# Output projection in eight pairs by seven products, and the down weight's sums made by accumulating transfers in DRAM

## The chip, the core and the metric

The kernel runs on one core of a Trainium2 chip. The metric is the device time of one execution in microseconds (us). Before the change three timed runs took 740.05, 740.07 and 741.11 us, median 740.07.

The engines are named as the profile names them: PE multiplies matrices (PEld loads its weights), DVE is the vector engine, ACT the activation engine, POOL the general engine, and SP issues most of the transfers. Each engine works through its own list of instructions in the order of the program, and waits where an operand is not ready. What stands behind a waiting instruction on the same engine waits with it.

## The reference, cut to what matters

The input `x` has 2048 rows of 640. After a layer norm it goes through two branches:

```
xn  = layernorm(x)
qkv = xn @ wqkv                  # 32 heads of 20, window of 8 positions, dilation 2
o   = windowed attention(qkv)    # 2048 x 640
s   = o @ wo                     # the output projection
h   = (xn @ w_gate) * (xn @ w_up)   # 2048 x 1536
g   = silu(h @ w_down)           # the down projection
out = x + s * g
```

All is float32. For PE each operand is cut into a high and a low part, and a product is the sum of three (high by high, high by low, low by high).

## The kernel before, in words

The rows are cut into sixteen tiles of 128 (NT = 16). The work goes through PE in this order: the query/key/value products beside the first gate and up products (to about 272 us), the gate and up products in groups (to about 520 us), the output projection (520 to 586 us), and the down projection (586 us to the end). Attention itself runs on DVE and POOL beside the products of the first two parts, and its results `o` go to DRAM, as do `h` and later `s`.

**Seven products instead of eight.** Where two tiles are taken together as a pair, rows and the inner dimension are halved into blocks A11, A12, A21, A22, the weight into B11 to B22, and a scheme of seven block products with sums S1 to S4 of the A blocks and T1 to T4 of the B blocks gives the four output blocks. `pair_product(p, j)` (line 1035) does product `j` of pair `p` of the output projection, `product(m)` (line 900) product `m % 7` of a pair of tiles of the down projection. The order of the seven is `H_IN` and `W_IN` (lines 771 and 772): A11 by B11, S1 by T1, S2 by T2, S4 by B22, S3 by T3, A12 by B21, A22 by T4. They use three banks of PSUM, `"ACACABA"`: the products 0, 2, 4 and 6 add onto bank A, 1 and 3 onto C, 5 has B. ACT copies the bank out after products 0, 1 and 2 (line 1050), and DVE adds such a copy to the bank after products 3, 4 and 5 (lines 1053, 1056, 1058). So product 3 must wait for the copy after product 1, product 4 for the copy after product 2, and product 6 for DVE's addition after product 4. The store of a pair's first tile goes out on SP behind the addition after product 5 (line 1059). The first product of the next pair is put between products 5 and 6.

The inner dimension of the output projection is five blocks of 128. Four make the scheme, and the fifth is added to the products 3 to 6 (`FIFTH`), so that six of a pair's 54 matrix instructions stand in each of the products 0 to 2 and nine in each of the products 3 to 6.

**The output projection before** has two parts. Tiles 0 to 9 go as five pairs (lines 1530 to 1578). For the next pair DVE turns the two tiles and forms S1, S2, S4, S3 (`turn_pair`, line 990), ACT makes the high parts (`hi_pair`, line 1001), DVE the low parts (`lo_pair`, line 1024), each in three parts: part 0 for A11 and A12, part 2 for S1, S2, S4, part 1 for S3 and A22. Tiles 10 to 15 go one by one without the scheme (`out_proj`, line 756): two halves of 15 matrix instructions each.

**The down weight before** is prepared beside this. `load_wd` (line 795) loads two row blocks, `sum_wd` (line 802) forms T1 to T4 on DVE with four subtractions per row block pair, and `split_wd` (line 825) cuts each of the seven blocks into high parts on ACT and low parts on POOL (`split`, line 112), 128 x 320 each, 42 in all. The first loads go out ahead of the output projection, each later one when POOL has ended the splits of the pair before (line 1526).

**The first `h` tiles** for the down projection are loaded in four pieces while tiles 12 and 13 are projected (lines 1588 to 1591). `hi_h`, `lo_h` and `sum_h` (lines 867, 871 and 850) make their high parts (ACT), low parts and sums (DVE).

SP works through its loads and stores in the order of the program too. A load waits on SP until the buffer that it writes is free.

Of the kernel before, what the change touches and what calls it, by code (L numbers as in the profile page):

```python
# [19 lines left out]
P = 128  # L20
# [22 lines left out]
SP = 10  # L43
# [13 lines left out]
def kernel(  # L57
# [183 lines left out]
    s_scr = dr.tile([NT, P, D], F32, name="s_scr")  # L241

# [469 lines left out]
    o_t, oT = {}, {}  # L712
# [14 lines left out]
    one_t = []  # L727

    def turn_o(s):
        if not one_t:  # L730
            one_t.append(slot([P, 2, KD, P], F32))
        y = one_t[0][:, s % 2]
        turn(y, s)
        return y

    def trans_o(s, amid):
        split_o(s, turn_o(s), amid)

    def split_o(s, y, amid=lambda: None):

        if s == NT - 2:
            oT[s] = st([P, KD, P], "gh", 5, F32R), st([P, KD, P], "gh", 5, F32R)
        else:
            if s == SP:
                z = blocks(wd_big[3], 4, 2, KD)
            else:
                z = slot([P, 2, KD, P]) if s < NT - 2 else st([P, 2, KD, P], "t", 2, F32R)
            oT[s] = z[:, 0], z[:, 1]
        hi, lo = oT[s]
        nc.scalar.activation(hi, y, AF.Copy)  # L750
        amid()
        nc.vector.tensor_sub(lo, y, hi.bitcast(F32))

    y_t = {}

    def out_proj(s, n):
        a = oT[s]
        if n == 0:
            y_t[s] = st([P, D], "gh", 5)
        c = slice(n * HALF, (n + 1) * HALF)  # L760
        p = pt([P, HALF], "q", 3)
        mm3(p, [([t[:, k, :] for t in a], [t[:, c] for t in wo_s[k]]) for k in range(KD)])
        nc.scalar.activation(y_t[s][:, c], p, AF.Copy)
        if n:
            oT.pop(s)
            nc.sync.dma_start(s_scr[s], y_t.pop(s))


    KH = KF // 2
    wd_raw, wd_t = {}, {}  # L770
# [3 lines left out]
    wd_big, wd_kv = [], {}  # L774

    def begin_wd(kv=None):

        if kv:
            y = wd_kv[kv] = st([P, KH - 1, 2, HALF], "kv", 2, F32R)
            wd_t[kv] = [y[:, k] for k in range(KH - 1)]  # L780
            if kv == "B22":
                for n, t in enumerate(("T4", "B22")):
                    wd_t[t].append(wd_big[0][:, KH + n])
            return
        y = st([P, KH + 2, 2, HALF], "xc", NCH, F32R)
        wd_t[("B11", "T1", "T2", "B21")[len(wd_big)]] = [y[:, k] for k in range(KH)]
        wd_big.append(y)
        if len(wd_big) == NCH:
            wd_t["T3"] = [wd_big[b][:, k] for b, k in ((2, 6), (2, 7), (3, 7), (3, 6), (1, 6), (1, 7))]
# [5 lines left out]
    def load_wd(k):  # L795
        wd_raw[k] = st([P, 2, 2, HALF], "wraw", 2)
        for a in range(2):
            nc.sync.dma_start(wd_raw[k][:, a].rearrange("p a c -> p (a c)"), wd[:, a * KH + k, :])

    wd_v = {}  # L800

    def sum_wd(k, part, half):
        r = wd_raw[k]
        if (part, half) == (0, 0):
            v = wd_v[k] = {"B11": r[:, 0, 0], "B21": r[:, 1, 0], "B22": r[:, 1, 1]}
            if k == 4:
                t = st([P, 3, HALF], "q", 1)
                v["T1"], v["T2"], v["T4"] = (t[:, i] for i in range(3))
            else:
                v["T1"], v["T2"] = st([P, HALF], "lg", 2), st([P, HALF], "lg", 2)  # L810
            nc.vector.tensor_sub(v["T1"], r[:, 0, 1], r[:, 0, 0])
        elif part == 0:
            v = wd_v[k]
            nc.vector.tensor_sub(v["T2"], r[:, 1, 1], v["T1"])
        elif half == 0:
            v = wd_v[k]
            if k != 4:
                v["T4"] = st([P, HALF], *(("gh", 5) if k < 3 else ("pk", 1)))
            v["T3"] = r[:, 0, 1]
            nc.vector.tensor_sub(v["T3"], r[:, 1, 1], r[:, 0, 1])  # L820
        else:
            v = wd_v[k]
            nc.vector.tensor_sub(v["T4"], r[:, 1, 0], v["T2"])

    def split_wd(k, part):
        for name in (("B11", "B22", "T1"), ("B21", "T2", "T3", "T4"))[part]:
            split(nc.gpsimd, wd_v[k][name], *(wd_t[name][k][:, i] for i in range(2)))
        if part:
            wd_raw.pop(k), wd_v.pop(k)
# [3 lines left out]
    def load_h(n, names=()):  # L833

        a, b = 2 * n, 2 * n + 1
        if n % 2:
            ta, tb = st([P, KF, P], "t", 2), st([P, KF, P], "t", 2)
            nc.sync.dma_start(ta, h_scr[a])
            nc.sync.dma_start(tb, h_scr[b])
            h_raw[n] = {"A11": ta[:, :KH], "A12": ta[:, KH:], "A21": tb[:, :KH], "A22": tb[:, KH:]}  # L840
        else:
            h_raw.setdefault(n, {})
            for name, s, k, tag, m in (("A11", a, 0, *(("wraw", 2) if n else ("s", SLOTS))), ("A21", b, 0, "s", SLOTS), ("A12", a, KH, "o", 1),
                                       ("A22", b, KH, "wraw", 2)):
                if names and name not in names:
                    continue
                h_raw[n][name] = st([P, KH, P], tag, m)
                nc.sync.dma_start(h_raw[n][name], h_scr[s][:, k:k + KH])

    def sum_h(m):  # L850
# [3 lines left out]
        if name == "S1":  # L854
            y = slot([P, 2, KH, P], F32)
            v["S1"], v["S2"] = y[:, 0], y[:, 1]
            nc.vector.tensor_add(v["S1"], v["A21"], v["A22"])
        elif name == "S2":
            nc.vector.tensor_sub(v["S2"], v["S1"], v["A11"])
        elif name == "S4":  # L860
            v["S4"] = slot([P, KH, P], F32)
            nc.vector.tensor_sub(v["S4"], v["A12"], v["S2"])
# [37 lines left out]
    def product(m):  # L900
# [8 lines left out]
        for r, (i, l, k) in enumerate(runs):  # L909
            nc.tensor.matmul(p, y[:, i, k], wd_t[name][k][:, l], start=new and r == 0, stop=r == len(runs) - 1,  # L910
                             skip_group_check=True)

    def gather(m):
# [10 lines left out]
        elif j == 3:  # L924
            g_t[a] = slot([P, D], F32)
            nc.vector.tensor_add(g_t[a][:, HALF:], kept["U2"], p)
            return lambda: silu(a, 1)
        elif j == 4:
            g_t[b] = slot([P, D], F32)
            nc.vector.tensor_add(g_t[b][:, HALF:], kept["M5"], p)  # L930
# [59 lines left out]
    def turn_pair(p):  # L990
# [8 lines left out]
        nc.vector.tensor_sub(a21, a11, a21)  # L999

    def hi_pair(p, part):

        if part == 2:
            if p % 2 or p > 3:
                z = slot([P, 2, 3 * KS, P])
                z = [z[:, 0], z[:, 1]]
            else:
                z = blocks(wd_kv["T4"], 2, 2, 3 * KS) if p else blocks(wd_big[0], 1, 2, 3 * KS)
                z = [z[:, 0], z[:, 1]]
            raw = pair_raw[p]  # L1010
        else:
            y, r = (wd_big[3], 3) if p % 2 else (wd_kv["T4"], 1) if p == 0 else (wd_kv["B22"], 2 if p == 2 else 4)
            if p > 3 and part:
                y, r = wd_big[2], 2
            if (p, part) in ((2, 1), (4, 0)):
                z = st([P, 2, KD, P], "pk", 1, F32R)
            else:
                z = blocks(y, r + 2 * part, 2, KD)
            z = [z[:, i] for i in range(2)]
            raw = pair_y[p][:, part]  # L1020
# [378 lines left out]
    last, BLOCK = len(MADE) - 1, (3, 4, 6, 8, 10)  # L1399
    RATE = ((1.0, 0.4), (0.3, 0.2), (0.4, 0.6), (0.8, 0.8))  # L1400
    for m, t in ((m, t) for m in range(1, len(MADE)) for t in range(DIL)):
# [3 lines left out]
        for i in range(NE):  # L1405
# [7 lines left out]
            if (m, r, i) == (last - 1, 1, 6):  # L1413
                load_wf(2)
            qkv(m, r, i)
# [25 lines left out]
    def begin_last():  # L1441
        advance(1e9)
        wo_keep.extend([load_wo((0, 1)), load_wo((2, 3)), load_wo((4,))[:, 0]])
        begin_wd("T4")
# [39 lines left out]
    split_t("T1", wd_big[0], 4)  # L1484
    split_t("T2", wd_big[0], 6)
# [8 lines left out]
    split_t("T3", wd_big[1], 4)  # L1494
    split_t("T4", wd_big[1], 6)
    load_wd(0)
    load_wd(1)
# [11 lines left out]
    wd_steps = [(k, part) for k in range(KH) for part in range(2)]  # L1509

    to_split = []

    def wd_sums(halves=(0, 1)):
        for half in halves:
            if half == 0 and wd_steps:
                to_split.append(wd_steps.pop(0))
            elif half == 0:
                return
            sum_wd(*to_split[-1], half)

    def wd_splits():
        while to_split:
            k, part = to_split.pop(0)
            split_wd(k, part)
            if part and k + 2 < KH:
                load_wd(k + 2)

    load_pair(3)
    pair_product(0, 0)
    for p in range(SP // 2):  # L1530
        more = p + 1 < SP // 2
        if p < 3:
            wd_sums()
        pair_product(p, 1)
        if more:
            hi_pair(p + 1, 0)
            lo_pair(p + 1, 0)
            if p == 3:
                wd_sums()
        else:  # L1540
            split_o(SP, y1)
        pair_product(p, 2)
        if not more:
            wd_splits()
            wd_sums()
        elif p < 3:
            hi_pair(p + 1, 2)
        pair_product(p, 3)
        if more:
            if p == 3:  # L1550
                hi_pair(p + 1, 2)
            hi_pair(p + 1, 1)
        pair_product(p, 4)
        wd_splits()
        if more:
            lo_pair(p + 1, 2)
        pair_product(p, 5)
        if more:
            lo_pair(p + 1, 1)
        if p == 0:  # L1560
            load_pair(4)
            turn_pair(2)
        elif p == 1:
            turn_pair(3)
        elif p == 2:
            load_o(SP, 3, st([P, 3, D], "t", 2))
            turn_pair(4)
        else:
            if p == 3:
                load_o(SP + 3, 3, st([P, 3, D], "t", 2))  # L1570
                y1 = turn_o(SP)
# [99 lines left out]
```

## Time and profile before

| what | us |
|---|---|
| median of three timed runs | 740.07 |
| profiled execution, from first to last instruction (the span) | 738.5 |
| timed median less span: what lies around it | 1.57 |
| PE busy in the span | 731.9 |
| DVE busy | 624.4 |
| POOL busy | 455.0 |
| ACT busy | 302.4 |

The page names no other time for the profiled execution than its span. How to read it: a timeline row holds the start and the duration of an instruction (or of several, merged, with their count), engine, line, operation, what it writes and reads, and in brackets how long the engine stood idle before it and on what. PE's matrix instructions overlap: the duration of one is about 0.31 us in this part, but the next one starts after half of that, so that a product's share of time is read from the start of one row to the start of the next. A DMA row gives line, count, size and the time from issue to landing.

### The profile page before, as it was taken

The numbers are of one execution on the slowest core, as the hardware profiler recorded it, in microseconds if no ns is written. First come the engines' busy times: TensorE is split into PE (matmuls) and PEld (weight loads), VectorE is DVE, ScalarE is ACT, GpSimd is POOL, SyncE is SP. The second block draws the span as 40 slices with busy tenths as digits, with TensorE's granted clock in tenths as the row PEclk, the third lists the DMA queues.
The fourth block names the chain that finished last, engine by engine and source line by source line (L and its number), as shares of the span: only waits on it lengthen the run. The fifth ranks groups of instructions, "written<-read, shape, count | busy, mean of one in ns | idle before, by whom it ended". The sixth has DMA issues, their size and how long they took to land.

```text
span 738.5 us, 11086 instructions
## 1 busy us (share of the span) xinstructions
PE 731.9 (99%) x4048; PEld 668.4 (91%) x4048; DVE 624.4 (85%) x729; ACT 302.4 (41%) x577; POOL 455.0 (62%) x384
## 2 busy tenths in 40 slices
PE   9999999999999999999999999999999999999997
PEld 7989989988999998888888888888999999999997
DVE  7676998899696989899989999968998777777775
ACT  5668312323232333233323332335566654444442
POOL 6159929887678889797879969577569700000000
PEclk9999999999999999999999999999999999999999
DMA  8465582867355649462634443278658655555534
GB/s 322 171 203 169 213 285 88 250 207 238 92 181 147 224 160 365 120 194 60 205 92 118 157 142 91 68 205 217 176 161 237 231 199 193 193 193 193 193 107 142
DMA packets 103491, 132.96 MB, mean 180 GB/s; under 512 B 22696, under 2 KB 74404, under 8 KB 103438
## 3 DMA queue, kind: packets, MB, share of 16 engines
q1 hardware_dynamic: 86286, 114.25, 48.9%
q10 hardware_dynamic: 16000, 12.78, 5.3%
q0 software_dynamic: 1152, 5.24, 2.1%
q8 instruction: 31, 0.51, 0.3%
q14 instruction: 22, 0.18, 0.1%
HBM read 83.58 MB, written 47.81 MB: 178 GB/s over the span
## 4 chain that ended last, share of the span: by engine, by line
PE 94%; DVE 2%; DMA 1%; issue 1%; POOL 1%; SPq 0%; ACT 0%; DVEq 0%; POOLq 0%
PE g L1340 14%; PE q L433 10%; PE u L1340 9%; PE q L910 9%; PE u L433 8%; PE g L433 8%; PE u L910 6%; PE q L1340 5%; PE u L124 5%; PE g L124 4%; PE g L910 3%; PE e L910 3%; PE q L124 2%; PE q L1047 2%; PE u L1047 1%; PE e L433 1%
## 5 line engine op out<-in xcount | busy, mean ns | idle before, releaser
L513 POOL TENSOR_TENSOR o<-o,t 128x960 f32<-128x960 f32 (+1 forms) x66 | 132.9, 2014 | 10.4 <-DVE t L507 9.6
L507 DVE TENSOR_TENSOR t<-e,kv 128x960 f32<-128x960 f32 (+1 forms) x96 | 99.5, 1038 | 16.1 <-POOL o L513 16.1
L541 DVE TENSOR_TENSOR t<-q,kv 128x1920 f32<-128x1920 f32 (+1 forms) x48 | 92.4, 1926 | 2.6 <-DMA kv<-qkv_scr 2.6
L548 DVE TENSOR_REDUCE lg<-t 128x96 f32<-128x1920 f32 (+1 forms) x48 | 92.3, 1922 | 0.2
L433 PE MATMUL q<-s,xc 128*128 128x360 f32 (+1 forms) x450 | 82.9, 334 | 0.3 <-DVE lg L271 0.2
L115 POOL TENSOR_TENSOR s<-wraw,s 128x384 fp32r<-128x384 f32 (+6 forms) x57 | 69.7, 1236 | 19.1 <-ACT s L114 19.1
L1309 ACT ACTIVATE gh<-g 128x512 f32<-128x512 f32 x57 | 34.2, 600 | 113.1 <-PE g L1340 108.6
L433 PEld LDWEIGHTS q<-s,xc 128*128 128x128 f32 x450 | 74.9, 188 | 4.4 <-DVE lg L271 0.5
L433 PE MATMUL u<-s,xc 128*128 128x360 f32 (+1 forms) x360 | 65.8, 334 | 0.0
L433 PEld LDWEIGHTS u<-s,xc 128*128 128x128 f32 x360 | 60.3, 188 | 2.3
L433 PE MATMUL g<-s,xc 128*128 128x360 f32 (+1 forms) x330 | 61.5, 337 | 0.0
L1340 PE MATMUL u<-xc,s 128*128 128x512 f32 x228 | 58.1, 390 | 0.0
L1340 PE MATMUL g<-s,s 128*128 128x512 f32 x228 | 58.0, 390 | 0.0
L433 PEld LDWEIGHTS g<-s,xc 128*128 128x128 f32 x330 | 55.7, 188 | 2.6
L910 PE MATMUL q<-xc,s 128*128 128x320 f32 x342 | 55.5, 309 | 0.0
L910 PEld LDWEIGHTS q<-xc,s 128*128 128x128 f32 x342 | 51.5, 188 | 0.0
L1340 PEld LDWEIGHTS u<-xc,s 128*128 128x128 f32 x228 | 42.8, 188 | 9.2 <-POOL s L115 0.3
L1340 PEld LDWEIGHTS g<-s,s 128*128 128x128 f32 x228 | 42.7, 188 | 9.1 <-ACT gh L1309 0.3
L114 ACT ACTIVATE s<-wraw 128x384 fp32r<-128x384 f32 (+6 forms) x58 | 32.6, 581 | 29.6 <-PE g L1340 10.2
L1340 PE MATMUL g<-xc,s 128*128 128x512 f32 x171 | 42.0, 390 | 0.1
L1340 PE MATMUL q<-xc,pk 128*128 128x512 f32 x171 | 41.8, 389 | 0.0
L513 POOL TENSOR_TENSOR o<-t 128x960 f32<-128x960 f32 (+1 forms) x11 | 22.1, 2014 | 27.9 <-DVE t L507 25.9
(365 smaller groups left out, 1564.5 us busy)
## 6 DMA issues: line engine op xcount, KB each, us to landing
h_scr<-gh SPq DMA_DIRECT2D x48, 256.0 KB, 2.6
wraw<-in_wgu SPq DMA_DIRECT2D x11, 640.0 KB, 4.4
kv<-qkv_scr SPq DMA_DIRECT2D x14, 480.0 KB, 5.6
t<-h_scr SPq DMA_DIRECT2D x8, 768.0 KB, 7.0
qkv_scr<-s ACTq DMA_DIRECT2D x17, 360.0 KB, 3.2
kv<-qkv_scr SPq DMA_DIRECT2D x14, 367.5 KB, 6.6
s_scr<-gh SPq DMA_DIRECT2D x16, 320.0 KB, 4.1
gh<-s_scr SPq DMA_DIRECT2D x16, 320.0 KB, 3.6
```

Of the source, the lines that this page charges most:

```text
L114: nc.scalar.activation(hi, raw, AF.Copy)
L115: eng.tensor_sub(lo, raw, hi.bitcast(F32))
L124: nc.tensor.matmul(acc, a, b, start=first and n == 0, stop=last and n == len(runs) - 1)
L433: nc.tensor.matmul(p, xT[(r * NE + i) // TPC][a][:, k, t0:t0 + P], wq[m][b][k], start=n == 0, stop=n == len(runs) - 1, skip_group_check=ac ...
L507: nc.vector.tensor_mul(t.rearrange("p (n d) -> p n d", d=DH), e[:, :, w].unsqueeze(2).to_broadcast([P, NE * nh, DH]), v)
L513: return NE * c * cost, lambda: eng.tensor_add(y, z, t)
L541: nc.vector.tensor_mul(t, q, k)
L548: nc.vector.tensor_reduce(out=lg[:, :, j:j + 2].rearrange("p n a -> p a n"), in_=t.rearrange("p a (n d) -> p a n d", d=DH), op=ALU.add, ax ...
L910: nc.tensor.matmul(p, y[:, i, k], wd_t[name][k][:, l], start=new and r == 0, stop=r == len(runs) - 1, skip_group_check=True)
L1047: nc.tensor.matmul(b, y, w, start=new and r == 0, stop=r == len(runs) - 1, skip_group_check=True)
L1309: nc.scalar.activation(kept[j], b["ACACABA"[j]], AF.Copy)
L1340: nc.tensor.matmul(y, w, x, start=j in (0, 1, 5) and r == 0, stop=r == len(runs) - 1, skip_group_check=True)
```

## The change

- All sixteen tiles go as pairs (`NP` = 8). `out_proj`, `split_o` and `load_o`'s groups of three tiles are gone.
- T1 to T4 of the down weight are formed in DRAM. Beside the query/key/value products SP copies four blocks of the weight into a scratch tensor, and POOL issues four transfers that add another block (or a sum already there) onto them, at five places (`W_SUMS`). Signs are turned so that all are additions; two sums of `h`, S1 and S4, and two additions after products change their signs to fit.
- The splits of the down weight are done from loaded blocks in larger pieces: two to four row blocks at once. They come in eight groups, each of which is loaded when the one before last is split, and are spread over the pairs by `EACH`. Three last groups overwrite places of the output projection's own weight sums, and so come in the last pair, each behind the product that used its place (`after`).
- For pairs 3 to 7 the sum S3 is formed on POOL.
- The `h` tiles of the first pair and two of the last groups are loaded behind product 5 of pair 6. Their high parts, low parts and sums stand between the products of pair 7.

```
@@ sums in DRAM
+    def wd_sum(n):
+        t = {name: w_scr[:, i] for i, name in enumerate(("T1", "T2", "T3", "T4"))}
+        if n == 0:
+            for name, b in (("T1", "B11"), ("T3", "B12"), ("T2", "B22"), ("T4", "B21")):
+                nc.sync.dma_start(t[name], wd_block(b))
+        else:
+            out, y = ((t["T1"], wd_block("B12")), (t["T3"], wd_block("B22")), (t["T2"], t["T1"]), (t["T4"], t["T2"]))[n - 1]
+            nc.gpsimd.dma_start(out, y, accum_op=ALU.add)
+    W_SUMS = ((1, 2), (1, 12), (2, 4), (2, 12), (3, 7))
...
+            if (m, n) in W_SUMS:
+                wd_sum(W_SUMS.index((m, n)))
             qkv(m, r, i)
@@ splits
+    def split_wd(u):
+        n = sum(len(ks) for _, ks in u)
+        y, r = w_row[u[0][0], u[0][1][0]]
+        split(nc.gpsimd, wd_raw.pop(u), *(y[:, r:r + n, l] for l in range(2)))
@@ turn_pair
-        nc.vector.tensor_sub(a21, a11, a21)
+        (nc.gpsimd if p > 2 else nc.vector).tensor_sub(a21, a11, a21)
@@ the loop over pairs
+    groups = [(unit("B11", 0, 1), unit("T1", 0, 1)), (unit("B22", 0, 1), unit("T3", 0, 1)), (unit("B11", 2, 3, 4, 5),),
+              (unit("T2", 0, 1), unit("B21", 0, 1)), (unit("T4", 0, 1), unit("B22", 2, 3)), (unit("T1", 2, 3, 4, 5),),
+              (unit("T2", 2, 3, 4), unit("B22", 4)), (unit("T2", 5) + unit("B22", 5),)]
+    last_groups = [(unit("T3", 2, 3), unit("T3", 4, 5)), (unit("B21", 2, 3, 4, 5),), (unit("T4", 2, 3, 4, 5),)]
+    EACH = (1, 2, 1, 2, 1, 1, 0, 0)
+    after = {1: last_groups[0][0], 2: last_groups[1][0], 4: last_groups[0][1], 6: last_groups[2][0]}
...
     load_pair(3)
     pair_product(0, 0)
+    wd_loads()
+    wd_loads()
+    for p in range(NP):
+        more = p + 1 < NP
+        def pair(j):
+            pair_product(p, j)
+            if not more and j in after:
+                split_wd(after[j])
+        if not more:
+            load_wd(last_groups[2], "pk", 1)
+        pair(1)
         if more:
             hi_pair(p + 1, 0)
             lo_pair(p + 1, 0)
+        if EACH[p] > 1:
+            wd_splits()
+        pair(2)
+        if more:
+            hi_pair(p + 1, 2)
+        else:
+            hi_h(0)
+            lo_h(0)
+            sum_h(1)
+        pair(3)
+        if more:
+            hi_pair(p + 1, 1)
+        else:
+            hi_h(1)
+            sum_h(2)
+        pair(4)
+        if EACH[p]:
             wd_splits()
         if more:
             lo_pair(p + 1, 2)
+        else:
+            lo_h(1)
+        pair(5)
         if more:
             lo_pair(p + 1, 1)
         if p == 0:
             load_pair(4)
+        elif p > 1 and p + 3 < NP:
+            load_pair(p + 3)
+        elif p == NP - 2:
+            load_h(0)
+            for group in last_groups[:2]:
+                load_wd(group)
+        if p + 2 < NP:
+            turn_pair(p + 2)
         if more:
             pair_product(p + 1, 0)
+        pair(6)
```

`wd_splits` splits the oldest loaded group and then loads the next one; `wd_loads` only loads.

More of the change, by code (lines that the diff above doesn't have):

```diff
@@ L791, in blocks, with wd_part @@
+        w_big.append(y)
+    def wd_part(name, k, l):
+        y, r = w_row[name, k]
+        return y[:, r, l]
     def blocks(y, r, h, n):
         return y[:, r:].rearrange("p r i c -> p (r i c)")[:, :h * n * P].rearrange("p (h n c) -> p h n c", h=h, c=P)
[L795 to L820, printed above, removed]
-        else:
-            v = wd_v[k]
-            nc.vector.tensor_sub(v["T4"], r[:, 1, 0], v["T2"])
@@ L909, in product @@
         for r, (i, l, k) in enumerate(runs):
[L910 removed]
+            nc.tensor.matmul(p, y[:, i, k], wd_part(name, k, l), start=new and r == 0, stop=r == len(runs) - 1,
                              skip_group_check=True)
```

213 lines of the change are left out of this document (58 added, 155 removed).

## The prediction

> **What bounds the kernel now.** I read the page first: span, busy times, and the chain that ended last.
>
> ```profile
> span 738.5 us, 11086 instructions
> ...
> PE 731.9 (99%) x4048; PEld 668.4 (91%) x4048; DVE 624.4 (85%) x729; ACT 302.4 (41%) x577; POOL 455.0 (62%) x384
> ...
> PE 94%; DVE 2%; DMA 1%; issue 1%; POOL 1%; SPq 0%; ACT 0%; DVEq 0%; POOLq 0%
> ```
>
> PE is the chain: the kernel is as long as PE's list plus whatever makes PE wait. So I ask how much PE work goes, and whether a new wait reaches PE. Next the windows (window, length, then PE, PEld, DVE, ACT, POOL busy, granted clock, DMA share, GB/s):
>
> ```profile
> 550.00:560.00 10.00, 10.00 (x70) 10.00 (x69) 9.66 (x14) 5.58 (x14) 9.36 (x9) 1.00 0.67 187
> ...
> 590.00:600.00 10.00, 10.00 (x71) 10.00 (x70) 8.62 (x12) 7.60 (x11) 0.00 (x0) 1.00 0.97 380
> ```
>
> PE has no gap here, at full clock; DVE and POOL are nearly full as well. DMA engines 0.97 busy moved 380 GB/s, which I take as their rate. Then PE's timeline in the pairs, and from the chain two halves of a tile done without the scheme:
>
> ```profile
> 519.69 1.04 PE L1047 MATMUL q<-s,kv 128*128 128x320 f32 x6
> ...
> 552.24 1.04 PE L1047 MATMUL u<-xc,s 128*128 128x320 f32 x6
> 553.12 1.04 PE L1047 MATMUL e<-xc,s 128*128 128x320 f32 x6
> 554.00 1.04 PE L1047 MATMUL u<-s,s 128*128 128x320 f32 x6
> ...
> 555.32 1.04 PE L1047 MATMUL e<-xc,xc 128*128 128x320 f32 x6
> ```
>
> ```profile
> 566.04 4.40 PE q L124 x30
> ```
>
> Products 1 to 4 of pair 4 start here. Six matrix instructions step by 0.88, nine by 1.32, thirty by 4.40: 0.1467 each. A pair takes 3 x 0.88 + 4 x 1.32 = 7.92.
>
> **What goes.** Six tiles alone are 6 x 2 x 15 = 180 matrix instructions, three pairs are 3 x 54 = 162. The 18 that go are 18 x 0.1467 = 2.64 us, all on the chain. DVE's 24 subtractions for the down weight and 12 loads go as well; PE never waited for them (10.00 of 10), so I cost that at nothing.
>
> **The sums in DRAM.** No row shows a copy from DRAM to DRAM or an accumulating one. The places are (1,2), (1,12), (2,12) and (3,7) in PE's timeline, (2,4) between; beside them SP's last issue before the copies, a POOL issue, and DVE's longest wait in that stage:
>
> ```profile
> 109.90 2.56 PE L433 MATMUL u<-s,xc 128*128 128x360 f32 x15
> ...
> 133.90 2.56 PE L433 MATMUL q<-s,xc 128*128 128x360 f32 x15
> ...
> 182.50 3.41 PE L433 MATMUL g<-s,xc 128*128 128x480 f32 x15
> ...
> 212.30 2.56 PE L433 MATMUL q<-s,xc 128*128 128x360 f32 x15
> ```
>
> ```profile
> 111.78 0.38 SPq L671 DMA_DIRECT2D h_scr<-gh  x1
> 124.13 0.35 SPq L148 DMA_DIRECT2D wraw<-in_wqkv  x1
> ```
>
> ```profile
> 263.66 0.76 POOL L1196 DMA_DIRECT2D s<-t_scr  x1
> ```
>
> ```profile
> 202.10 0.56 DVE L575 TENSOR_REDUCE sm<-e 128x48 f32<-128x384 f32 x1 [5.89 <-ACT e L570]
> ```
>
> The four copies are 128 x 1920 x 4 = 0.98 MB each, 3.93 MB, 10.3 us at 380 GB/s; SP has nothing to issue from 112 to 124, so the next load meets an emptied queue, or, if bytes count twice, one emptied by 133, where the first sum is due. The four POOL issues are 0.76 each, 3.0 us; what stands behind them on POOL is attention's additions, and DVE waits for those. Three lie ahead of DVE's 5.89 of slack at 202; the fourth may delay DVE by 0.8. Bounds: 0 to +2 us on PE; I take 0. [...]
>
> **First wait: the first group of splits.** SP issues its two loads behind the four of pair 3; and the same size of load later shows its landing:
>
> ```profile
> 522.73 0.38 SPq L1298 DMA_DIRECT2D h_scr<-gh  x1
> 523.21 2.14 SPq L718 DMA_DIRECT2D t<-o_scr  x4
> ```
>
> ```profile
> wraw<-in_wd SPq DMA_DIRECT2D x2, 320.0 KB, 3.4
> ```
>
> ```profile
> 524.35 0.45 ACT L114 ACTIVATE xc<-wraw 128x320 fp32r<-128x320 f32 x1
> ```
>
> They issue at 525.35 and 525.8 and land about 528.9 and 529.7 (the second 0.84 later, 328 KB at 380 GB/s). ACT's first split of pair 0 stood at 524.35, and it stands there still: ACT stops until the load has landed. Behind them on ACT stands the copy after product 0 of pair 1, which product 2 of pair 1 needs.
>
> ```profile
> 553.38 0.44 ACT L1050 ACTIVATE o<-u 128x320 f32<-128x320 f32 x1 [0.50 <-PE u L1047]
> 553.72 0.73 ACT L750 ACTIVATE xc<-s 128x640 fp32r<-128x640 f32 x1
> 554.34 0.43 ACT L1050 ACTIVATE o<-e 128x320 f32<-128x320 f32 x1
> ...
> 590.13 0.85 ACT L869 ACTIVATE s<-s 128x768 fp32r<-128x768 f32 x1 [0.64 <-DVE s L862]
> ```
>
> ACT takes 0.34 from start to start for 320 elements, 0.62 for 640. So the copy runs 530.35 to 530.8, and product 2 starts at 530.9. It was due 9.68 after 519.69 (0.88, then 2 x 0.88 + 3 x 1.32, then 0.88 + 1.32 + 0.88): 529.4. **+1.5** (0 if the loads were early, 2.5 if they queue longer).
>
> **Second wait: two groups a pair.** In pairs 1 and 3 a group stands behind product 1 as well. ACT's rows above: the copy after product 1 starts 1.14 after that product's start (0.26 after the next one's start), then the part 0 high parts 0.34 on, two splits of 0.62 in the new list, so the copy after product 2 starts 0.26 + 0.34 + 3 x 0.62 = 2.46 after product 2's start and ends at 2.9. Product 4 is due at 0.88 + 1.32 = 2.2 (553.12 to 555.32). **+0.7** for pair 1. For pair 3 the same, and I allow 0.5 more, since its part 0 high parts need transposes that stand on a nearly full DVE: **+1.2** (0.7 to 2). Another 0.3 I allow where larger POOL pieces hold DVE (next but one part).
>
> **Third wait: the last groups.** Let 0 be the end of product 5 of pair 6. DVE's addition, then SP's store, come first:
>
> ```profile
> 543.26 0.48 DVE L1058 TENSOR_TENSOR gh<-o,g 128x320 f32<-128x320 f32 x1
> ```
>
> ```profile
> 543.77 0.32 SPq L1059 DMA_DIRECT2D s_scr<-gh  x1
> ```
>
> Three loads issued 0.45 apart show what queueing does:
>
> ```profile
> s<-h_scr SPq DMA_DIRECT2D x1, 384.0 KB, 4.2
> ...
> s<-h_scr SPq DMA_DIRECT2D x1, 384.0 KB, 4.7
> ...
> o<-h_scr SPq DMA_DIRECT2D x1, 384.0 KB, 5.2
> ```
>
> Each landing is 0.5 later than its issue explains: data move one after the other, 1.0 per 393 KB, with about 3.2 around them, of which I put 1.4 behind the data. In the new list: store issued at 0.7, the two `h` tiles (786 KB each) at 1.15 and 1.6, T3 (2,3) at 2.05, T3 (4,5) at 2.5, B21 at 2.95. The data start at 2.0 and take 0.85, 2.05, 2.05, 0.85, 0.85, 1.7: T3 (2,3) lands at 7.8 + 1.4 = 9.2, B21 at 11.7. ACT wants T3 (2,3) behind product 1 of pair 7, which ends at 0.88 + 1.32 + 0.88 = 3.08, and stops until 9.2. Behind it is the copy after product 2, done at 9.2 + 0.62 + 0.44 = 10.3; product 4 needs that and was due at 3.08 + 0.88 + 1.32 = 5.28. **+5.0.** Below: if T3's load did not queue behind the others it would land at 2.05 + 3.4 = 5.45 and leave +1.3. Above: at 300 GB/s, +7.
>
> **Fourth wait: `h` between the products of pair 7.** Behind the copy ACT has B21's high part, four row blocks, 1280 elements: from 0.73 and 0.85 about 1.27, with 1.16 to the next start. So it runs from 11.7, the high part of A11 from 12.9 to 13.7. DVE stands at the low part of A11, and behind it S1 and only then the addition after product 3, then S2, then the addition after product 4, for which product 6 waits. POOL meanwhile splits B21. How DVE and POOL stand to each other, in their timelines:
>
> ```profile
> 432.49 2.37 DVE L1315 TENSOR_TENSOR gh<-gh,gh 128x512 f32<-128x512 f32 x1
> ...
> 484.20 0.68 DVE L1315 TENSOR_TENSOR gh<-gh,gh 128x512 f32<-128x512 f32 x1
> ...
> 588.27 0.96 DVE L873 TENSOR_TENSOR s<-s,s 128x768 fp32r<-128x768 f32 x1
> ```
>
> ```profile
> 432.06 2.25 POOL L513 TENSOR_TENSOR o<-o,t 128x960 f32<-128x960 f32 x1 [0.57 <-DVE t L507]
> ...
> 515.12 1.57 POOL L115 TENSOR_TENSOR s<-t,s 128x640 fp32r<-128x640 f32 x1
> ```
>
> The DVE instruction that starts behind a POOL instruction ends 0.55 after POOL's end (434.86 against 434.31) and takes 2.37 instead of 0.68: it is held while POOL's runs. 1280 elements on POOL are 1.57 + 2 x 0.68 = 2.9. POOL starts B21 at 13.0 and ends at 15.9; DVE's low part ends at 16.7, S1 at 17.5, the addition 17.9, S2 18.8, the addition 19.2. Product 6 was due at 10.3 + 2 x 1.32 = 12.9. **+6.3.** Below, without the hold and with early loads, 3.7. After that the low part of S2 (product 2 of the down projection) is late by about **0.3**. From there on PE's list is the same as before.
>
> **The sum.** -2.64 + 1.5 + 0.7 + 1.2 + 0.3 + 5.0 + 6.3 + 0.3 = +12.7. The span becomes 738.5 + 12.7 = 751.2; the median stood 1.57 above the span, so 752.8.
>
> **Rivals.** *Loads side by side.* If T3's load does not queue, the third wait is 1.3 and the fourth about 5.7, since B21 lands at 7.4 too: 12.7 - 3.7 - 0.6 = +8.4, 748.5. For it: the measured spacing is of three loads only. Against: 380 GB/s is all that the engines moved.
>
> *Everything hidden, faster.* Then only the 18 instructions count: 740.07 - 2.64 = 737.4. For it: before the change every load of this stage is hidden. It holds if the last groups land within 3 us of their issue; against it stands the shortest such row, 3.4, and one wait of over 2.64 already turns the sign.
>
> [...]
>
> **How the numbers follow.** About 0.2% (1.5 us) is what a measurement here can tell from no change. Forecast 752.8: 0.65. Side by side, 748.5: 0.2. POOL held: 0.04. Hidden, or nearly: 0.11, of which 0.08 faster and 0.03 within 0.2%. Slower: 0.89. The range goes from 745 (side by side, no hold on DVE, half of the small waits) to 758 (slow loads, +2 from the sums in DRAM); it leaves out the hidden case and the held POOL.
>
> **What would show it.** In the new profile: ACT's first split of pair 0 waits some 4 us for a load; product 4 of pair 7 starts some 5 us late behind ACT's split of T3, which waits for its load; product 6 of pair 7 waits some 6 us for DVE; the down projection has no new gaps; 18 fewer matrix instructions. Wrong would be: PE without gaps from 520 to 600, or gaps before 285 us.

## The result and the profile after

The changed kernel takes 759.13 us (median; 758.53 to 761.5), the kernel before 740.06 in the same session. The ratio is 1.0259, with a 95% interval of 1.024 to 1.0279: slower, by 19.1 us where 12.7 had been forecast, and above the upper end of the range, 758.

The page of the changed kernel:

```profile
span 759.7 us, 11016 instructions
...
PE 737.2 (97%) x4030; PEld 672.1 (88%) x4030; DVE 630.1 (83%) x724; ACT 302.2 (40%) x555; POOL 448.9 (59%) x368
...
PE 83%; DMA 4%; DVE 4%; POOL 3%; issue 3%; SPq 2%; ACT 1%; DVEq 0%; POOLq 0%; ACTq 0%
```

There are 18 matrix instructions fewer (4030 against 4048), as the change says, and yet PE is busy 5.3 us longer. PE has fallen from 94% to 83% of the chain; DMA, DVE, POOL and issuing have grown from 5% to 14%. PE's waits (engine, tile, line, what it waited for: us in total, times, longest):

```profile
PE e L993 <- ACT o L996: 9.9, 3, 4.7
PE e L993 <- DVE gh L1002: 4.2, 1, 4.2
PE q L993 <- ACT o L996: 1.6, 3, 0.9
```

All seven lie in the pairs, 15.7 us together (each one to two decimals: 3.52, 0.20, 0.88, 1.72, 0.54, 4.67, 4.18). The kernel before has none there. PE's timeline at the three long ones (start, us, instruction, count, in brackets the idle time before it):

```profile
528.68 1.04 PE L993 MATMUL u<-xc,s 128*128 128x320 f32 x6
533.25 1.97 PE L993 MATMUL e<-xc,s 128*128 128x320 f32 x6 [3.52 <-ACT o L996]
535.01 1.80 PE L993 MATMUL u<-s,s 128*128 128x320 f32 x6
536.61 1.00 PE L993 MATMUL u<-s,xc 128*128 128x320 f32 x3
...
540.86 1.04 PE L993 MATMUL q<-s,xc 128*128 128x320 f32 x6
...
594.97 1.97 PE L993 MATMUL e<-xc,s 128*128 128x320 f32 x6 [4.67 <-ACT o L996]
596.73 1.00 PE L993 MATMUL e<-s,s 128*128 128x320 f32 x3
597.53 2.60 PE L993 MATMUL g<-s,xc 128*128 128x320 f32 x9
604.31 1.97 PE L993 MATMUL e<-xc,s 128*128 128x320 f32 x6 [4.18 <-DVE gh L1002]
606.08 1.00 PE L993 MATMUL e<-q,s 128*128 128x320 f32 x3
606.88 3.06 PE L863 MATMUL q<-xc,s 128*128 128x320 f32 x18
```

Look at the second column. Six instructions stepped by 0.88 before; behind the long waits they step by 1.76 (533.25 to 535.01, 594.97 to 596.73), exactly twice that. The windows say why (window, length, busy times of PE, PEld, DVE, ACT, POOL, then the granted clock, DMA share, GB/s):

```profile
530.00:540.00 10.00, 6.75 (x28) 6.75 (x29) 3.92 (x8) 6.49 (x12) 6.45 (x4) 0.66 0.60 194
590.00:600.00 10.00, 5.33 (x20) 4.80 (x19) 1.30 (x1) 3.06 (x4) 3.54 (x2) 0.69 0.82 320
600.00:610.00 10.00, 5.82 (x30) 5.69 (x30) 7.88 (x9) 3.82 (x6) 4.48 (x3) 0.80 0.25 83
610.00:620.00 10.00, 10.00 (x70) 10.00 (x69) 9.09 (x9) 6.99 (x11) 1.77 (x1) 1.00 0.97 347
```

The granted clock, 1.00 in every window of 10 us from 520 to 590 in the kernel before, is 0.66 to 0.80 where PE has waited long. No term of the forecast had that. The engines behind the waits, ACT first:

```profile
523.91 0.72 ACT L968 ACTIVATE xc<-s 128x640 fp32r<-128x640 f32 x1
531.13 0.74 ACT L114 ACTIVATE xc<-wraw 128x640 fp32r<-128x640 f32 x1 [6.50 <-DMA wraw<-in_wd]
532.13 0.74 ACT L114 ACTIVATE xc<-wraw 128x640 fp32r<-128x640 f32 x1 [0.27 <-DMA wraw<-w_scr]
532.78 0.42 ACT L996 ACTIVATE o<-e 128x320 f32<-128x320 f32 x1
...
593.85 0.74 ACT L114 ACTIVATE xc<-wraw 128x640 fp32r<-128x640 f32 x1 [5.23 <-DMA wraw<-w_scr]
594.50 0.42 ACT L996 ACTIVATE o<-e 128x320 f32<-128x320 f32 x1
596.66 1.27 ACT L114 ACTIVATE xc<-wraw 128x1280 fp32r<-128x1280 f32 x1 [1.75 <-DMA wraw<-in_wd]
```

SP's issues of those loads:

```profile
525.70 0.46 SPq L778 DMA_DIRECT2D wraw<-in_wd  x1
526.26 1.95 SPq L778 DMA_DIRECT2D wraw<-w_scr  x1
...
587.52 1.18 SPq L778 DMA_DIRECT2D wraw<-w_scr  x2
```

And DVE ahead of the last wait:

```profile
598.70 3.03 DVE L826 TENSOR_TENSOR s<-t,s 128x768 fp32r<-128x768 f32 x1 [11.83 <-ACT s L822]
601.65 0.94 DVE L810 TENSOR_TENSOR s<-t 128x768 f32<-128x768 f32 x1
602.52 0.47 DVE L999 TENSOR_TENSOR gh<-o,u 128x320 f32<-128x320 f32 x1
602.92 0.94 DVE L812 TENSOR_TENSOR s<-s,t 128x768 f32<-128x768 f32 x1
603.78 0.47 DVE L1002 TENSOR_TENSOR gh<-o,e 128x320 f32<-128x320 f32 x1
```

This is the chain that had been forecast: ACT stops at a split whose load hasn't landed, the copy for PE stands behind it; in pair 7 DVE does the low part of A11 beside POOL's large piece (3.03 for what takes 0.95 alone), S1 and S2, and the addition for product 6 comes last.

**Where the 21.2 us of the profiled execution went.** The pairs take 519.89 to 606.88 = 86.99. Eight pairs without a gap are 8 x 7.92 = 63.36. The difference is 23.6: 15.7 of waits, 7 x 0.26 = 1.8 that a wait costs beyond its length (the last row ahead of it ends 0.16 after the next could have started, and at full clock the row behind it steps by 0.98 instead of 0.88, as from 597.14 to 598.12 in e5_late_fill below), and 6.1 of slow clock. Before, the pairs and tiles took 66.00, so the stage is 21.0 longer; it starts 0.20 later, and the down projection takes 148.3 against 148.1.

That execution took 761.5, 2.4 above the median; the spans of the four are 759.7, 756.7, 756.9 and 757.8. No trace shows where the other three were shorter.

### The profile page after: what moved, and what is told of

It reads as the page before. It is cut to its first block, busy times and chain, and to the rows that moved or that the text cites. A ratio compares the mean times of both kernels' runs of the same rounds, so it can differ in the third digit from the quotient of the medians.

```text
span 759.7 us, 11016 instructions
## 1 busy us (share of the span) xinstructions
PE 737.2 (97%) x4030; PEld 672.1 (88%) x4030; DVE 630.1 (83%) x724; ACT 302.2 (40%) x555; POOL 448.9 (59%) x368
## 4 chain that ended last, share of the span: by engine, by line
PE 83%; DMA 4%; DVE 4%; POOL 3%; issue 3%; SPq 2%; ACT 1%; DVEq 0%; POOLq 0%; ACTq 0%
PE g L1286 14%; PE q L434 10%; PE u L1286 9%; PE q L863 8%; PE u L434 8%; PE g L434 8%; PE u L863 6%; PE q L1286 5%; PE g L124 5%; PE u L124 4%; PE g L863 3%; PE e L863 3%; DMA wraw<-in_wd 2%; PE e L434 1%; POOL xc L115 1%
## 5 line engine op out<-in xcount | busy, mean ns | idle before, releaser
L115 POOL TENSOR_TENSOR xc<-wraw,xc 128x640 fp32r<-128x640 f32 (+1 forms) x11 | 23.0, 2099 | 30.9 <-ACT xc L114 30.9
```

Source lines behind the costliest of these rows:

```text
L115: eng.tensor_sub(lo, raw, hi.bitcast(F32))
```

## The experiments

Times are medians, with the ratio to the kernel before and its 95% interval. "The pairs" are the span from the first product of pair 0 to the first of the down projection, split as above: 63.36 + waits + 0.26 for each + the rest. Where PE has no slow stretch the rest is nearly nothing (0.04 in e12_reorder, 0.39 in e10_shift; 1.10 in e9_early_dve is the most), so a larger rest can be read as the price of the slow clock.

**e1_early: the first groups loaded early.**

```
     split_t("T4", w_big[1], 4)
+    wd_loads()
+    wd_loads()
     begin_wd()
...
     pair_product(0, 0)
-    wd_loads()
-    wd_loads()
```

> The first two groups of splits are loaded two unit-steps earlier, behind the splits of T3 and T4 of the output weight; nothing else moves. Three theories of the changed kernel's lost time. A (waits for loads and orders, and behind each wait of over 3 us a stretch at half the PE clock): the gap of 3.52 before product 2 of pair 1 goes, and the slow clock behind it with some 2.8; a short wait of up to 0.7 before product 4 of pair 1, now hidden by the slow clock, shows. 759.1 - 3.5 - 2.8 + 0.7 = 753.5, between 752.5 and 755. B (the same waits, but the slow clock comes from something else in this stage and stays): 759.1 - 3.5 + 0.5 = 756. C (the pairs hold too much work for DVE and POOL, so a wait that is taken away comes back at the next product): over 758.

Measured: 758.79, 1.0248 (1.0233 to 1.0263), 0.3 below the changed kernel's median. The long wait and its slow stretch went, and by the medians nearly all of it came back: PE waits 1.09, 0.24, 1.56, 0.86, 1.71 and 0.54 in pairs 1 to 5. Product 3 of pair 7 ends at 587.19; in e3_order, which has the late loads, at 587.45. In the changed kernel's own profile it ends at 590.29, but that execution lay 2.4 above its median. So by the times theory A was wrong for the pairs, and C right: the late load covered other delays, in pair 1 mostly ACT's two splits ahead of the copy after product 2, in pair 2 DVE.

**e2_late: the last groups loaded ahead of `h`.**

```
             load_wd(to_split[-1])
+        elif ahead:
+            load_wd(ahead.pop(0))
...
+    ahead = last_groups[:2]
...
             load_h(0)
-            for group in last_groups[:2]:
-                load_wd(group)
```

> The loads of T3 (2 to 5) and B21 (2 to 5) are issued as soon as a buffer is free, behind the groups of pairs 4 and 5, instead of behind the two tiles of h in pair 6. A: product 4 of pair 7 (594.97 now) starts without a wait at about 590.3; ACT does B21's high part at about 591.5 instead of 596.7, POOL its low part until some 595.6, DVE the low part of A11 until 596.4 and then S1, the addition, S2, the addition until 598.9; product 6 starts at about 599 instead of 604.3, with a wait of about 5. The time falls by 4.5 to 5.5, to 754.2. C: what holds product 6 is DVE and POOL beside each other whatever the loads do; product 6 stays at about 604 and the time at 758 or more.

Measured: 754.16, 1.0189 (1.017 to 1.0207). Product 4 of pair 7 has no wait, product 6 waits 4.27 for DVE. The mechanism is A's. That the median is A's to the tenth is in part luck: product 6 starts 7.1 behind product 4 (587.94 to 595.02), where A had 8.7.

**e3_order: `h` behind one addition.**

```
             hi_h(0)
-            lo_h(0)
-            sum_h(1)
         pair(3)
...
-            hi_h(1)
-            sum_h(2)
+            lo_h(0)
+            sum_h(1)
         pair(4)
+        if not more:
+            hi_h(1)
+            sum_h(2)
```

> On DVE the low part of A11 and S1 stand behind the addition after product 3 of pair 7, S1's high part and S2 behind the addition after product 4; the loads stay. A: the wait of 4.18 before product 6 goes, product 4 still waits 4.7 for T3; products 4 and 5 run slow as before, product 6 follows product 5 at about 600.2, and the down projection starts at about 602 to 602.7 instead of 606.9: 759.1 - 4.7 = 754.4 (753.5 to 755.5). C: the low part of A11, held by POOL until 601.7, and S1 behind it become what products 0 and 1 of the down projection wait for: 757 or more.

Measured: 759.48, 1.025 (1.0233 to 1.0267). A miss of mine, not a finding on the theories. DVE's timeline:

```profile
595.79 3.04 DVE L826 TENSOR_TENSOR s<-t,s 128x768 fp32r<-128x768 f32 x1 [3.41 <-ACT s L822]
598.76 2.28 DVE L810 TENSOR_TENSOR s<-t 128x768 f32<-128x768 f32 x1
600.96 0.47 DVE L1002 TENSOR_TENSOR gh<-o,e 128x320 f32<-128x320 f32 x1
```

Product 6 needs the addition after product 4 (line 1002), and the low part and S1 still stood ahead of that one.

**e4_fill: work in the gaps.**

```
+        if (p, j) in FILL:
+            f = pt([P, HALF], "g", 2)
+            for r in range(FILL[p, j]):
+                nc.tensor.matmul(f, *runs[r % len(runs)], start=r == 0, stop=r == FILL[p, j] - 1, skip_group_check=True)
...
+    FILL = {(1, 1): 18, (7, 3): 24, (7, 5): 40}
```

> Matrix instructions are added whose result nobody reads: 18 behind product 1 of pair 1, 24 behind product 3 and 40 behind product 5 of pair 7, 82 x 0.1467 = 12.0 us of PE work at full clock, in the three places where PE waits long. Everything else is as in the changed kernel. A (a long gap costs clock afterwards): the waits end where they ended, but the six or so instructions behind them run at 0.88 per six instead of 1.76: behind the first wait 2.8 less, of which 0.7 comes back before product 4; behind the second nothing, since product 6 waits for DVE anyhow; behind the third 1.4 less. 759.1 - 3.5 = 755.6 in spite of the added work (754.5 to 757). B (the slow clock is not caused by the gap): the clock stays low there, and the added instructions, which at half clock take up to 24 us, push the work behind them: 759 to 771.

Measured: 760.15, 1.0265 (1.0243 to 1.0287). By its time, inconclusive, since only the first of the three amounts fitted. There product 2 of pair 1 ran at full clock (1.14 for six instead of 1.97), as A says. At the second, T3's load landed only at 594.5, so that 3.98 of waiting and the slow clock were left; at the third the 40 instructions ended 2.2 after DVE. The next run does it in one place.

**e5_late_fill: one gap, filled.**

```
e2_late, and
+    FILL = {(7, 5): 26}
```

> The kernel with the loads of T3 and B21 ahead of h (e2_late), and behind product 5 of pair 7, where PE waits 4.27 for DVE, 26 matrix instructions more whose result nobody reads: 26 x 0.1467 = 3.8 us of added work in the one long wait that is left there. A (a long gap halves the clock for a while): product 6 still starts at the same time, but takes 1.32 instead of 2.56, and product 0 of the down projection 2.64 instead of 3.9: 754.2 - 2.5 = 751.7, though PE has more to do. B (the slow stretch has another cause): 754.2, or some more.

Measured: 751.94, 1.0154 (1.0139 to 1.017); e2_late had 1.017 to 1.0207. Adding 26 matrix instructions made the kernel 2.2 us faster: its runs took 751.17 to 752.91, those of e2_late 753.21 to 756.6. PE in e2_late:

```profile
595.02 1.97 PE L993 MATMUL e<-xc,s 128*128 128x320 f32 x6 [4.27 <-DVE gh L1002]
596.78 1.01 PE L993 MATMUL e<-q,s 128*128 128x320 f32 x3
597.58 4.07 PE L863 MATMUL q<-xc,s 128*128 128x320 f32 x18
601.49 2.80 PE L863 MATMUL u<-xc,s 128*128 128x320 f32 x18
```

and in e5_late_fill:

```profile
592.67 3.98 PE L998 MATMUL g<-s,xc 128*128 128x320 f32 x26
597.14 1.14 PE L994 MATMUL e<-xc,s 128*128 128x320 f32 x6 [0.50 <-DVE gh L1007]
598.12 0.60 PE L994 MATMUL e<-q,s 128*128 128x320 f32 x3
598.56 2.80 PE L863 MATMUL q<-xc,s 128*128 128x320 f32 x18
601.20 2.07 PE L863 MATMUL u<-xc,s 128*128 128x320 f32 x13
```

The same instructions, waiting for the same addition, take 4.06 up to product 1 of the down projection where PE had worked (597.14 to 601.20), and 6.47 where it had stood (595.02 to 601.49). So at this place the slow stretch is the price of the gap, not of the stage.

**e6_tail: `h` behind both additions.**

```
e2_late, and for pair 7 (moved there from behind products 2 to 4)
         pair(4)
+            lo_h(0)
+            sum_h(1)
+            hi_h(1)
         pair(5)
+            sum_h(2)
+            lo_h(1)
```

> e2_late, and the low part of A11 and S1 stand on DVE behind the addition after product 4 of pair 7 (e3_order had them behind the addition after product 3 only, which product 6 doesn't need), S1's high part behind them, S2 behind product 5. A: the wait of 4.27 before product 6 goes and the slow stretch of 2.5 behind it; the low part of A11 is done at about 592.5 and product 0 wants it at about 593.7: 754.2 - 6.8 = 747.4 (746.5 to 749). C: DVE, held by POOL's splits, is late for products 0 and 1 of the down projection instead: over 751.

Measured: 752.19 (749.35 to 754.43), 1.0144 (1.012 to 1.0169): between the theories. The wait before product 6 is gone, but DVE, held by POOL's pieces (2.12, 2.33 and 3.51 for instructions of 0.95), is late for products 1 to 3 of the down projection, 0.94 + 1.10 + 0.93. The last two of these:

```profile
604.27 0.99 PE L863 MATMUL q<-kv,s 128*128 128x320 f32 x5 [1.10 <-DVE s L826]
...
606.34 1.35 PE L863 MATMUL u<-kv,s 128*128 128x320 f32 x5 [0.93 <-ACT lg L840]
```

In this execution the clock fell behind three short waits (0.83 from 605 to 615); in e7_tail_nosums the same three waits left it at 1.00.

**e7_tail_nosums: without the sums in DRAM.**

```
e6_tail, and
-    W_SUMS = ((1, 2), (1, 12), (2, 4), (2, 12), (3, 7))
+    W_SUMS = ()
...
-                b = w_scr[:, int(name[1]) - 1] if name[0] == "T" else wd_block(name)
+                b = wd[:, int(name[1]) - 1] if name[0] == "T" else wd_block(name)
```

> e6_tail without the copies and the accumulating transfers in DRAM; the loads of T1 to T4 read blocks of the down weight as they are, so the output is that of other weights and everything else is the same work. If the sums in DRAM cost PE nothing: the same as e6_tail within 0.7. If their traffic or POOL's four issues do cost: up to 2 less than e6_tail.

Measured: 751.8, 1.0148 (1.013 to 1.0166): the same as e6_tail within what the two scatter (749.57 to 752.81 and 749.35 to 754.43), so the times alone would not show a cost of 1 us. In their profiles the pairs start at 519.35 here and at 519.32 with the sums.

**e8_tail_dve and e9_early_dve: the low parts on DVE.**

```
e6_tail, and (e8)
             for u in to_split.pop(0):
-                split_wd(u)
+                split_wd(u, nc.vector)
and in e9 also the early loads of e1
```

> e6_tail with the low parts of the splits in pairs 0 to 5 on DVE instead of POOL. C says that the waits left in the pairs (some 6 us) come from DVE, which POOL's splits hold: from 535 to 580 in e3_order, POOL was busy 27.7 us and DVE's instructions took 12.8 us more than the shortest of their form. On DVE the same 8320 elements take 8320 x 0.73 / 640 = 9.5 us. So DVE gains up to 3 us and the time falls by 1 to 3 against e6_tail. If DVE isn't held by POOL so much as by its own list and by what it waits for, its list is 9.5 us longer and the time rises by 2 to 8.

> e8_tail_dve with the first two groups loaded early, as in e1_early. In e8_tail_dve product 1 of pair 2 comes 4.89 late, because DVE stands in order behind the first splits, whose loads land at 530.7 and 531.8, and the clock is low behind that (0.82 from 535 to 545, 1.8 us); DVE's instructions take their bare times there. A: with early loads all of that goes and nothing comes back, since DVE is no longer held by POOL: 754.3 - 4.9 - 1.8 = 747.6 (746.5 to 749.5). C in its stronger form (DVE's own list is too long for the pairs, whoever holds it; in e1_early six waits came back): over 751.

Measured: e8 754.32, 1.0184 (1.0169 to 1.02); e9 748.28, 1.0107 (1.0092 to 1.0122). e8 alone was a miss, since DVE now stands in order behind the first splits, whose loads are late: a wait of 4.89. With the loads early the time falls by 6.0 us, and this time little comes back (waits of 0.83 and 0.34 in pairs 1 and 2). The same low parts of a pair, on DVE, in e1_early (splits on POOL; count, then ns min/median/max):

```profile
L972 DVE TENSOR_TENSOR s<-s,s x3: 945/1789/2720, 537.1 to 566.5; 128x640 fp32r<-128x640 f32 x2, 128x768 fp32r<-128x768 f32 x1
L972 DVE TENSOR_TENSOR pk<-s,pk x3: 1786/3187/3189, 538.3 to 575.2; 128x640 fp32r<-128x640 f32 x3
```

and in e9_early_dve:

```profile
L972 DVE TENSOR_TENSOR s<-s,s x3: 818/819/955, 537.6 to 566.9; 128x640 fp32r<-128x640 f32 x2, 128x768 fp32r<-128x768 f32 x1
L972 DVE TENSOR_TENSOR pk<-s,pk x3: 811/820/820, 538.9 to 575.1; 128x640 fp32r<-128x640 f32 x3
```

0.82 alone, 3.19 beside POOL's 1280 elements. Early loads were worth 0.3 us where the splits' low parts were on POOL (e1_early), and 6.0 where they were on DVE; but in e8 the late load stops DVE itself, so the two are not the same loss. No run has early loads, e6's order and the low parts on POOL; with the 0.3 of e1 it would take about 751.9, an estimate, so that DVE instead of POOL is worth some 3.6 in e9. The waits in the pairs fall from 7.78 (e6_tail) to 3.61 (e9).

**e10_shift and e11_all_dve: the last splits.**

```
e9, and (e10)
-    after = {1: ..., 2: last_groups[1][0], 4: ..., 6: last_groups[2][0]}
+    after = {1: ..., 4: ...}
...
+        if m in (0, 2):
+            split_wd(last_groups[1 + m // 2][0])
+            if m == 0:
+                load_h(1)
or (e11)
-                split_wd(after[j])
+                split_wd(after[j], nc.vector)
```

> e9_early_dve, and the splits of B21 and T4 stand behind products 0 and 2 of the down projection instead of between the products of pair 7, the loads of h for the second pair behind the first of them. In e6_tail and e8_tail_dve products 1, 2 and 3 of the down projection wait 0.9 to 1.1 each: POOL's low parts hold DVE's work on h. A: these waits go, 3.0 less than e9_early_dve, some 744.6. Rival: POOL holds DVE just as long some products later, and there is no slack of four products any more: no less than e9_early_dve, or some more.

> e9_early_dve, and the last splits (T3, B21, T4 in pair 7) have their low parts on DVE too, so that POOL does nothing there and holds nothing. 4 x 0.73 x 2 = some 5 us more on DVE's list, where held instructions take 2.12, 2.33 and 3.51 instead of 0.95 (5.1 us). A: DVE ends as early or earlier, and the short waits of products 1 to 3 of the down projection become shorter: e9_early_dve less 1 to 3, some 745.5. Rival: DVE stands behind ACT's high part of B21 in order and the additions for products 5 and 6 come late: e9_early_dve plus 1 to 3.

Measured: e10 746.97, 1.009 (1.0077 to 1.0104); e11 745.8, 1.0073 (1.0061 to 1.0085). e11 is faster than e9 by 2.5, as A says. Of e10's 3.0 only 1.3 came, and its interval overlaps e9's: a wait of 1.63 for DVE appears at 608. In e11 POOL has no split left in this stage, and of the three waits at the down projection one of 0.67 is left.

**e12_reorder and e13_spread: what is left.**

```
e11, and (e12)
         pair(1)
...
-        if EACH[p] > 1:
-            wd_splits()
         pair(2)
...
         pair(3)
...
+        if EACH[p] > 1:
+            wd_splits()
         pair(4)
-        if EACH[p]:
-            wd_splits()
-        if more:
-            lo_pair(p + 1, 2)
...
         pair(5)
         if more:
+            lo_pair(p + 1, 2)
+            if EACH[p]:
+                wd_splits()
             lo_pair(p + 1, 1)
and in e13 also
-    EACH = (1, 2, 1, 2, 1, 1, 0, 0)
+    EACH = (2, 1, 1, 1, 1, 1, 1, 0)
```

> e11_all_dve, and the order within a pair is changed: the first group's splits and the low part of S1, S2, S4 stand behind the addition after product 5 instead of ahead of it, the second group's behind product 3 instead of product 1. In e11_all_dve nine of the waits in the pairs, 4.0 us, are for ACT's copies after product 0 (which come late because the place they write to is still to be read by the addition after product 5, and that stands on DVE behind splits) and after product 2 (behind two high parts on ACT); each wait costs some 0.26 more than the trace lists, 1.14 + 0.16 instead of 0.88 + 0.16 for its first row and the row ahead of it. If order is what costs: up to 4.0 + 9 x 0.26 = 6.3 less, say 4, some 742. If DVE's list is what costs (it is busy 9.0 to 9.9 of 10 there with no instruction held), other waits take their place: 745 or more.

> e12_reorder with the groups of splits spread evenly: two in pair 0, then one a pair to pair 6, instead of 1, 2, 1, 2, 1, 1. In e12_reorder the two pairs with two groups hold the longest waits (1.35 and 1.77 for the addition after product 4, and 0.59 in the pair behind each), where DVE is busy 9.5 to 9.9 of 10 with nothing holding it. If DVE's list in single pairs is what is left of the loss, these 4.3 us and 4 x 0.26 go and pair 0 gets back about 1: 746.1 - 4.3 = 742 (741 to 743.5). If something else makes these waits (the copies on ACT, the loads), they come in other pairs: 745 or more.

Measured: e12 746.13, 1.0076 (1.0062 to 1.0089); e13 745.4, 1.007 (1.0056 to 1.0084). By order alone nothing is won: the waits for ACT's copies shrink, and waits for DVE's addition take their place, in the two pairs with two groups, such as this one:

```profile
556.66 1.15 PE L993 MATMUL q<-xc,s 128*128 128x320 f32 x6 [1.77 <-DVE gh L1002]
```

Spread evenly, these waits go as expected, to 0.16 to 0.23 a pair and 0.66 once, and DVE is busy 9.8 of 10 from 525 to 575. But a wait of 1.69 for DVE comes in pair 7, and the time falls by 0.7, within the scatter of the two, where 4 had been expected (the profiled execution, 743.35, was the fastest of the five). That DVE's own list is what is left fits these rows but isn't proved by the time. None of the versions beats the kernel before; 745.4 is the best.

## Why the prediction was wrong

The direction and the chain of three of the four waits came as forecast; the amount did not. Term by term, for the profiled execution:

| term | forecast | measured |
|---|---|---|
| what goes | -2.64 | -2.64 |
| later start of the pairs (sums in DRAM) | 0 | +0.20 |
| first wait | +1.5 | +3.52 |
| second wait, ACT's splits in pairs 1 and 3 | +1.9 | +0.88 |
| POOL's larger pieces (pairs 2, 4 and 5) | +0.3 | +2.46 |
| third wait | +5.0 | +4.67 |
| fourth wait | +6.3 | +6.44 |
| low part of S2 | +0.3 | 0 |
| beyond a wait's length, 7 x 0.26 | none | +1.82 |
| slow clock behind the waits | none | +4.08 |
| sum | +12.7 | +21.4 (the spans: 21.2) |

The fourth wait's 6.44 are the 4.18 that stand in the trace and 2.26 by which products 4 and 5 were slow; had they been quick, product 6 would only have waited longer. So of the slow clock's 6.1 in the pairs 2.67 and 1.15 count, and 0.26 in product 0 of the down projection.

**The step that failed is the sum.** It adds the lengths of the waits to PE's list, as if PE went on at full speed behind them. Two terms are missing, 1.82 and 4.08, or 5.9 of the 8.7 us of error in this execution; by the medians the forecast is 6.3 short. e5_late_fill shows the larger of them by itself, at one place. Two terms are also mis-sized, each by some 2 us: the landing in the first wait, and the 0.3 for POOL's larger pieces.

What the traces show of the slow clock: in the changed kernel PE ran at half its pace (1.76 against 0.88, 0.50 granted from 533.3 to 539.0) for about 5.8 us from 533.25. The length of the gap alone doesn't fix when the clock falls: in e2_late and e3_order waits of 2.78 and 2.82 sufficed, in e7_tail_nosums one of 2.36 did not, and in e5_late_fill PE took its first six instructions behind a wait of 3.51 at full pace (0.97 from 533.46 to 534.43) before it slowed (0.85 granted from 535 to 545). In e6_tail the clock fell behind three waits of about 1 close together, in e7_tail_nosums, with the same three, it did not. The runs of a kernel scatter with it: e6_tail's 754.43, 753.2, 751.19 and 749.35 have mean granted clocks of 0.992, 0.996, 0.997 and 0.999.

**First wait: mechanism right, size off.** The landing was put at 3.4 after the issue, from a row of a quiet queue (issued at 537.54 in the kernel before, with 0 GB/s moved from 537.0 to 538.5). Behind pair 3's four loads the two took some 5.4 and 5.9 (525.70 to 531.13 and 526.26 to 532.13, the starts of the splits), and the issue of the second held SP for 1.95. So ACT stood still for 6.50, not some 4.

**Second wait: ACT's part right, POOL's far too small.** Both parts hold product 4, by the copy after product 2. In pair 3 the copy, at 555.09, stands behind two splits on ACT, as forecast, and PE waits 0.88. In pair 1 the slow stretch covers that wait; it is 1.09 in e1_early, and 0.83 and 0.82 are left in pairs 1 and 3 of e9_early_dve, where POOL does none of these splits. In pairs 2, 4 and 5 no split stands there. The copy stands behind a high part, that one behind DVE's transposes, and those behind a low part which POOL's piece holds. Pair 4, where PE waits 1.72:

```profile
559.83 3.05 POOL L115 TENSOR_TENSOR xc<-wraw,xc 128x1280 fp32r<-128x1280 f32 x1 [0.59 <-ACT xc L114]
...
560.38 3.18 DVE L972 TENSOR_TENSOR pk<-s,pk 128x640 fp32r<-128x640 f32 x1
...
563.48 1.56 DVE L725 STREAM_TRANSPOSE s<-t 128x640 f32<-128x640 f32 x2
...
564.35 0.74 ACT L968 ACTIVATE xc<-s 128x640 fp32r<-128x640 f32 x1 [2.27 <-DVE s L725]
```

This is the term set at 0.3; with 0.20 and 0.54 in pairs 2 and 5 it is 2.46, and in e9_early_dve product 4 of these three pairs waits no more (waits of 0.34 to 0.44 ahead of products 1 and 2 are what its pairs 2 to 5 have besides pair 3's 0.82). e1_early shows besides that the first two waits are no two terms to be added: without the first the pairs lose nearly as much by the medians, since the other delays lie beside the late load.

**Third and fourth wait: right**, within 0.33 and 0.14, the queueing of the loads included; the rival of loads side by side (1.3) is out. In the fourth the low part was let end 0.8 behind POOL's piece where the rows shown gave 0.55; it ended 0.82 behind it (600.91 to 601.73). e2_late takes the third wait away, e6_tail the fourth.

**The sums in DRAM: right.** SP issued the copies in 2.64 at 113.11, POOL the four sums in 1.06, 0.75, 0.56 and 0.56; PE has no new gap from there to 520, and e7_tail_nosums is no faster beyond the scatter. The later start of 0.20 lies ahead of the copies: PE's wait at 8.6 is 0.68 where it was 0.22. T2's sum, issued at 186.25, had landed by 197.9 (11.6 at most), and T4's, which reads it, was issued at 219.82. POOL's row ahead of each of the four issues ends as the issue starts, without a gap, so the sums held POOL nowhere, and the held POOL, given 0.04, is out.

**Everything hidden** is out by 3.52, 4.67 and 4.18.

## What to carry to other kernels

Price a gap of the bounding engine at more than its length: here each cost 0.26 beyond it, and behind every one of 2.78 us or more PE ran at half clock for some us (1.76 instead of 0.88 for six instructions in the changed kernel). Filling such a gap with useless work was faster than waiting where the amount fitted (751.94 in e5_late_fill, 754.16 in e2_late), and not where it didn't (760.15 in e4_fill, 759.13 in the changed kernel). When work on POOL runs beside a nearly full DVE, count it on DVE too (here 3.19 instead of 0.82 for a low part), and try it on DVE itself. Before two waits on different engines are added up, ask whether the one lies beside the other; taking one away by itself (e1_early) is the test.

## What had not been expected of the hardware

- The clock behind gaps, as above: 0.66 to 0.80 granted in windows of 10 us of the changed kernel.
- Low parts of 640 elements took 0.82 on DVE alone (e9_early_dve) and 3.19 beside a piece of 1280 on POOL (e1_early); a piece of 1280 on DVE took 1.48 (e9_early_dve), so that DVE lost more by waiting beside POOL (2.37) than by doing the piece itself.
- The accumulating transfers cost little to issue (0.56 to 1.06) and 7.8 to 11.6 to land for 0.98 MB, in the changed kernel's trace.
